# A delta-rule recurrence with a soft mixture of experts: each PSUM bank to one engine at a time in the plan, and half of the query masks by ScalarE and GpSimd

## The chip, the cores and the metric

The kernel runs on one core of one Trainium2 chip. The metric is the device time in microseconds (us) of one execution. The engines are TensorE (PE in the profile; its weight loads are PEld), VectorE (DVE), ScalarE (ACT), GpSimd (POOL) and SyncE (SP), which issues nearly all DMAs. Each engine works through its own queue in order; semaphores tie the queues together. TensorE writes to PSUM, which has 8 banks of 512 float32 columns on 128 partitions; everything else lives in one SBUF tile.

## The reference, cut to what matters

```python
# attention: batch 4, heads 8, 768 tokens, head size 48
k_n = k / (norm(k) + 1e-6)
for t in range(S):
    y[:, :, t] = einsum('bhd,bhde->bhe', q[:, :, t], state)
    v_old = einsum('bhde,bhd->bhe', state, kt)
    state = state + bt * einsum('bhd,bhe->bhde', kt, vt - v_old)
# soft mixture of experts on x (3072 x 384): 8 experts, 4 slots each, F = 1024
logits = x @ phi
d = softmax of logits over the tokens;  slot_input = d.T @ x
slot_out[e] = maximum(slot_input[e] @ w1[e], 0) @ w2[e]
c = softmax of logits over the slots;   out = c @ slot_out
```

## The kernel before

The recurrence is worked in 12 chunks of 64 tokens, all 32 heads together. Two chunks make a pair g (0 to 5). For a chunk n:

- `load_kq`, `load_v` (L470, L485) bring K, Q and V. `turn` (L535) transposes them on TensorE, eight 128x128 blocks at a time, and L546 copies the result out of PSUM.
- `gram` (L560) multiplies keys with keys, and keys with queries, per head. Its output tile has two banks, one for each index i. `keys` copies the key part out with a mask (ScalarE L587 and L585; VectorE L583 for the lower part of chunks 0 and 1); `queries` masks the query part on VectorE (L600) into `AT`. For chunks below `APART` = 4 keys and queries have tiles of their own, later ones share one tile for each half of the heads. `pack` (L625; VectorE for chunks 0 and 1, else GpSimd) gathers the diagonal blocks of the pair in `Gd`.
- `invert(g)` inverts the 16x16 diagonal blocks of the pair on VectorE: a transpose (L677), the norms of the keys (L690, Ln and Exp on ScalarE L694 and L695, reciprocals L707 and L709, small products on GpSimd L700 to L706), a scaling (L717), 15 columns of a multiply and a subtract (L727, L731), and transposes back (L749, L757). GpSimd spreads the result (L766).
- `join(n)` builds the inverse of the 64x64 block: L793, products L802, L820, L853, L864 with their copies L810, L826, L832, L843, L856, L869, and at the end the fix of the far part, L874 (`fix64`), into `Zs`.
- `step(n)` is the recurrence: `ks` (L910) reads the state, L917 subtracts from V, `qs` (L929) gives the first part of Y, `w` (L942) is the solution U, which ScalarE copies to `cU` (L956). GpSimd copies its second half with the partition halves exchanged to `cU2` (L962), because in `AT` the heads of the second half lie on the other partitions. `sup` (L982) adds to the state in PSUM (`pS`, two banks of its own), ScalarE copies it out (L988), and `au` (L1003) adds the second part of Y, copied out by L1013. In the last step the U copies are split between ScalarE and VectorE by partition half, each over its 384 columns (L956, L966), and Y is made in two parts.
- `route(n)` transposes Y (L1038, copy L1045) and makes the slot logits (L1063, copy L1069). `phase` (L1111 to L1152) keeps a running softmax over the tokens and adds up the slot inputs (L1141, L1150); it runs after chunks 3, 7, 10 and 11.

After the last step come `top` and `t3` (L1242, the slot inputs turned), the first expert products (`first`, L1267, with relu L1274 and L1276 and transposes L1283), the second ones (L1300), and for each half of the columns the sum over experts (L1311) and the product with the combine weights (L1322), copied out by L1324 and stored by L1326. `combine(g)` makes these combine weights: a transpose (L1081), a softmax (L1085 to L1094) and a transpose back (L1096, copy L1098). The weights of the experts are loaded by L1207 (w1) and L1217 (w2).

No order is written by hand. `Plan` collects every operation with its engine, an assumed duration, and the buffers it reads and writes. `schedule` is a list scheduler that runs at build time: it keeps a clock for each engine, takes the ready operation whose remaining path plus `key` is largest, gives it addresses in SBUF and PSUM, and emits the operations in the order of their assumed start. `SHIFT` adds a number to the key of each kind of operation; `SLACK` lengthens the path of one copy of the state (L988, upper half). `after=` in `op` orders an operation in the plan without any data behind it. Where the plan expects TensorE to be idle, it puts a filler product (L453) into a spare bank: `pl.spare` names the state's banks until the state is first written, later a bank must be free. The semaphores that the program really waits on are derived from what the emitted instructions read and write, banks of PSUM included, not from the plan's clock.

Of the kernel before, what the change touches and what calls it, by code (L numbers as in the profile page):

```python
# [16 lines left out]
SLACK = 0.00  # L17
HEAD = 40.0
SHIFT = {
    0: -43.2, 1: 38.7, 2: 22.3, 3: 23.9, 4: -10.2, 5: 9.8, 6: -5, 7: 3.3, 8: 43.6, 9: -36.4,  # L20
    10: -3.7, 11: -70.3, 12: -18.3, 13: -15.3, 14: 18, 15: 69.1, 16: -83.2, 17: 34.4, 18: 17.4,
    19: -17, 20: -10, 21: -21.3, 22: -80.1, 23: -24.9, 24: -39.6, 25: 33.2, 26: 46.2, 27: -4.5,
    28: -53.6, 29: 26.6, 30: 3.1, 31: 116.3, 32: -19.1, 33: 72.8, 34: -27.9, 35: 43, 36: -12.6,
    37: 27.4, 38: 21.6, 39: 25.9, 40: 38.2, 41: -12.1, 42: -52.9, 43: 39.8, 44: 1.5, 45: -59.4,
    46: 13.1, 47: 11.7, 48: -54.3, 49: -6.2, 50: -27.4, 51: -21.7, 52: 29.9, 53: 29.9, 54: 25.4,
    55: -86.9, 56: -75.3, 57: -1.3, 58: 40.6, 59: 2.6, 60: 52.3, 61: -1, 62: 67.4, 63: -21.5,
    64: 22.5, 65: 6.7, 66: -2.6, 67: -23.8, 68: 23.2, 69: -36.6, 70: -61.2, 71: -15.8, 72: 20.5,
    73: 6.7, 74: -41.5, 75: 10.7, 76: 35.5, 77: 5.4, 78: -50.1, 79: 17.8, 80: 9.7, 81: -3.2,
    82: -26.6, 83: 3.5, 84: -32.5, 85: 17.6, 86: 49.6, 87: -45.4, 88: 19.9, 89: -10, 90: 40.2,
    91: -5.8, 92: 0.9, 93: -0.8, 94: 15.1, 95: 11.2, 96: -14.5, 97: 10.1, 98: -8.6, 99: -89.6,  # L30
    100: -11.5, 101: -13.4, 102: -12.3, 103: -17.7, 104: -1.7, 105: -15.2, 106: 3.4, 107: 20,
    108: 11.8, 109: 2, 110: -1.4, 111: -52.5, 112: 10.9, 113: 31.5, 114: -40.9, 115: -2.6,
    116: -46.4, 117: -32.5, 118: -6.7, 119: -62.2, 120: 45.1, 121: -27.1, 122: 3.7, 123: -25.1,
    124: 2.8, 125: -25.9, 126: -75.6, 127: 27.6, 128: 83.5, 129: 62.8, 130: 32.4, 131: 55.6,
    132: 26, 133: -75.5, 134: -118.6, 135: -56.5, 136: 63.1, 137: 73.4, 138: -3.2, 139: -5,
    140: -7.2, 141: -54.1, 142: -41.2, 143: 6.1, 144: 77.3, 145: 22.9, 146: -19.4, 147: 20.7,
    148: -48.2, 149: 44.3, 150: 17.8, 151: 27, 152: 62.3, 153: 14.5, 154: -12.8, 155: -21.7,
    156: 10.5
# [13 lines left out]
class Op:  # L52
    def __init__(self, eng, dur, fn, lat, key):
        self.eng, self.dur, self.fn, self.lat, self.key = eng, dur, fn, lat, key
        self.deps, self.outs, self.bufs = {}, [], {}
        self.start = self.done = None
        self.path = self.slack = 0.0
        self.port = False

# [58 lines left out]
class Plan:  # L118
# [22 lines left out]
    def op(self, eng, dur, fn, r=(), w=(), after=(), lat=0.0, key=0.0, keep=0, ni=8, ut=300.0, port=False):  # L141
# [10 lines left out]
        for mode, regs in (("r", r), ("w", w)):  # L152
            for reg in regs:
                b, part = reg if isinstance(reg, tuple) else (reg, None)
                b.uses.append((o, part, mode))
        for a in after:
            if a is not None:
                o.deps[a] = None
# [16 lines left out]
    def schedule(self):  # L175
# [3 lines left out]
        live = {False: [], True: []}  # L179
        wait = {o: len(o.deps) for o in self.ops}  # L180
# [20 lines left out]

        busy = {"DVE": 0.0, "POOL": 0.0}
# [3 lines left out]
        while left:  # L206
# [13 lines left out]
            for x in cand:  # L220
                o = x[1]
                t = max(free[e], x[0])
                new = [b for b in o.bufs if b.addr is None]
# [20 lines left out]
                if e == "PE":  # L244

                    while self.filler:
# [9 lines left out]
                        b.addr = self.spare[0].addr if self.spare[1].start is None else room(b, at, 0)  # L256
# [19 lines left out]
                order.append(o)  # L276
                left -= 1
# [30 lines left out]
def kernel(  # L308
# [18 lines left out]
    P = 128  # L327
# [246 lines left out]
    def keys(n, j0, nj, ps, w):  # L574
        def ev(y, lower):
            dve = lower and n < 2

            def go():
                i_ = A(ps).rearrange("p i (y j f) -> p i y j f", j=4, f=w)[:, :, y - j0 // 4, :, 0:C].rearrange(
                    "p i j (b t) -> p i j b t", b=2)  # L580
                o = G3(n)[:, 8 * y:8 * y + 8].rearrange("p (i j) b t -> p i j b t", i=2)
                if dve:
                    nc.vector.tensor_scalar(o[:, :, :, 1], i_[:, :, :, 1], M1(), None, op0=ALU.mult)  # L583
                elif lower:
                    nc.scalar.activation(o[:, :, :, 1], i_[:, :, :, 1], ACT.Copy, scale=M1())  # L585
                else:
                    nc.scalar.activation(o[:, :, :, 0::2], i_, ACT.Copy, scale=M0())  # L587
            pl.op("DVE" if dve else "ACT", (t_dvp(256) if dve else t_act(256)) if lower else 0.60, go, r=[ps, cm0],
                  w=[(Gk[n], (lower, y))])
        for y in range(j0 // 4, (j0 + nj) // 4):  # L590
            ev(y, 0)
            ev(y, 1)
# [3 lines left out]
    def queries(n, j0, nj, ps, w):  # L596
        x = lambda: A(ps).rearrange("p i (y j f) -> p i y j f", j=4, f=w)[:, :, 0:nj // 4, :, w - C:w]
        for y in range(nj // 4):
            def cut(y=y):
                nc.vector.tensor_tensor(  # L600
                    x4(A(AT[n]), j0, nj, C)[:, :, y], x()[:, :, y],
                    A(cmA).unsqueeze(1).unsqueeze(1).broadcast_to([P, 2, 4, C]), op=ALU.mult)
            pl.op("DVE", 0.70, cut, key=-50, r=[ps, cmA], w=[(AT[n], y + j0 // 4)])
# [51 lines left out]
    def invert(gs):  # L655
# [51 lines left out]
        pl.op("DVE", 0.25, lambda: V.reciprocal(A(rn), A(nrm)), r=[nrm], w=[rn])  # L707
        pl.op("POOL", 0.89, norm, r=[ssq], w=[nrm, rn], port=True)
        pl.op("DVE", 0.25, lambda: V.reciprocal(A(rn), A(nrm)), r=[nrm], w=[rn])  # L709
# [173 lines left out]

    cS, cU, cU2 = pl.buf(32 * D), pl.buf(32 * D), pl.buf(16 * D)
    for t in (cU, cU2, cS):
        pl.op("POOL", t_ps(t.size), lambda t=t: nc.gpsimd.memset(A(t), 0.0), w=[t], key=20)

    def step(n):
# [58 lines left out]
        U2 = lambda: A(cU2).rearrange("p (i j f) -> p i j f", i=2, j=4)  # L947
        last = n == N - 1

        def uev(c):  # L950
            def go():
                o = A(cU).rearrange("p (y x c d) -> p y x c d", y=2, c=2, d=D)[ha(c), :, :, c]
                x = A(pW)[ha(c), :, 0:8 * D].rearrange("p y (x d) -> p y x d", d=D)
                if last:
                    o, x = o[:, 0], x[:, 0]
                (nc.vector.tensor_copy if c and last else nc.scalar.copy)(o, x)  # L956
            return go

        def uev2(c):
            def go():  # L960
                if not last:
                    nc.gpsimd.tensor_copy(  # L962
                        A(cU2).rearrange("p (x c d) -> p x c d", c=2, d=D)[ha(c ^ 1), :, c],
                        A(cU).rearrange("p (y x c d) -> p y x c d", y=2, c=2, d=D)[ha(c), 1, :, c])
                    return
                (nc.vector.tensor_copy if c and last else nc.scalar.copy)(  # L966
                    A(cU2).rearrange("p (x c d) -> p x c d", c=2, d=D)[ha(c ^ 1), :, c],
                    A(pW)[ha(c), 1, 0:8 * D].rearrange("p (x d) -> p x d", d=D))
            return go
        for f, b, cols in ((uev, cU, 384 if last else 768), (uev2, cU2, 384)):  # L970
            for c in H2:
                if b is cU2 and not last:
                    pl.op("POOL", t_po(384), f(c), r=[(cU, c)], w=[(b, c)], port=True)
                    continue
                dve = c and last
# [383 lines left out]
```

## Time and profile before

| | |
|---|---|
| median of 3 runs | 290.08 us (289.23 to 290.38) |
| profiled execution | 289.64 us, of which the span is 287.9 us |
| mean granted TensorE clock | 0.966 |
| start of solution L942 of chunk 0, 1, 2, 3 | 48.65, 64.33, 84.75, 99.0 us |
| of chunk 4, 5, 6, 7 | 120.08, 138.64, 152.25, 175.21 us |
| of chunk 8, 9, 10, 11 | 188.04, 201.08, 216.88, 226.80 us |
| t3 (L1242) ends, last L1300 starts, last output is issued | 240.05, 270.70, 284.3 us |

The span is cut in 40 equal slices; each digit is the busy share of a slice in tenths, and PEclk is the granted TensorE clock in tenths of full speed:

```profile
PE   8998899698988989989998989988897999999870
DVE  3789989778768957998769877987241387320440
PEclk9999999799999999999999999999999997999965
DMA  8999954808509293370766601489999999999596
```

VectorE is full in the early slices and fills again whenever a pair is inverted; after slice 27 it is mostly idle. DMA is full in the first slices (K, Q and V of the first chunks) and from slice 27 on (the experts' weights). The clock drops in slice 8, in the expert products, and at the end.

### The profile page before, as it was taken

The page shows a single profiled execution, that of the slowest core. Times are in us where ns is not written, and L with a number is a line of the kernel's source. Part 1 is how long each engine was busy: PE and PEld are TensorE (multiplying, and loading weights), DVE is VectorE, ACT ScalarE, POOL GpSimd, SP SyncE. Part 2 cuts the span into 40 slices and gives each one's busy share as a digit, 9 for nine tenths or more (in the row PEclk, how much of TensorE's full clock was granted, in tenths as well). Part 3 has the DMA queues.
Part 4 walks back from the last instruction along what each step waited for, and adds up shares of the span by engine and source line. Part 5 has one row for each costly group of instructions (what it writes and reads, how often), then busy time and mean ns, then how long its engine had stood idle before and what let it go on. Part 6 is the DMA issues. An engine that isn't in the chain of part 4 may idle for free.

```text
span 287.9 us, 13776 instructions
## 1 busy us (share of the span) xinstructions
PE 252.9 (88%) x6040; PEld 212.5 (74%) x6040; DVE 191.6 (67%) x438; ACT 149.8 (52%) x279; POOL 119.3 (41%) x288
## 2 busy tenths in 40 slices
PE   8998899698988989989998989988897999999870
PEld 6887788697878878688888879877786764367650
DVE  3789989778768957998769877987241387320440
ACT  5484386358557486359656856563645352201430
POOL 8943058705943377715952677417422000000000
PEclk9999999799999999999999999999999997999965
DMA  8999954808509293370766601489999999999596
GB/s 103 141 138 138 137 82 59 124 4 106 65 5 123 46 133 40 59 112 3 91 80 77 93 2 31 109 203 338 384 355 297 318 315 322 329 305 314 170 293 223
DMA packets 105836, 45.12 MB, mean 157 GB/s; under 512 B 77009, under 2 KB 99569, under 8 KB 105777
## 3 DMA queue, kind: packets, MB, share of 16 engines
q1 hardware_dynamic: 105600, 44.05, 71.1%
q8 instruction: 47, 0.77, 1.2%
q10 hardware_dynamic: 48, 0.10, 0.2%
q0 software_dynamic: 128, 0.10, 0.2%
q14 instruction: 13, 0.10, 0.2%
HBM read 39.52 MB, written 4.72 MB: 154 GB/s over the span
## 4 chain that ended last, share of the span: by engine, by line
PE 37%; DVE 30%; POOL 10%; issue 7%; ACT 7%; DMA 5%; SPq 1%; DVEq 0%; ACTq 0%; POOLq 0%
DVE sb L727 6%; DVE sb L731 5%; PE pb L1267 4%; PE pb L1300 4%; PE pb L1322 3%; DVE sb L832 3%; PE pb L535 3%; PE pb L982 3%; PE pb L929 3%; DMA sb<-in_q_dram 2%; POOL sb L843 2%; POOL sb L625 2%; DVE sb L600 2%; POOL sb L766 2%; DMA sb<-in_k_dram 2%
## 5 line engine op out<-in xcount | busy, mean ns | idle before, releaser
L843 POOL COPY sb<-sb 32x128 f32<-32x128 f32 x96 | 30.2, 315 | 19.7 <-DVE sb L826 12.2
L546 ACT ACTIVATE sb<-pb 128x1024 f32<-128x1024 f32 x23 | 22.9, 1023 | 10.7 <-PE pb L535 10.4
L766 POOL COPY sb<-sb 32x256 f32<-32x256 f32 x44 | 19.6, 445 | 20.3 <-DVE sb L757 18.4
L731 DVE TENSOR_TENSOR sb<-sb 128x30 f32<-128x30 f32 (+7 forms) x90 | 25.8, 287 | 3.1
L727 DVE TENSOR_TENSOR sb<-sb 128x30 f32<-128x30 f32 (+7 forms) x90 | 26.2, 291 | 2.4
L560 PE MATMUL pb<-sb 48*64 48x128 f32 (+1 forms) x1024 | 25.7, 247 | 1.7 <-DVE sb L600 1.1
L535 PE MATMUL pb<-sb 128*128 128x128 f32 x192 | 24.6, 276 | 1.8 <-DMA sb<-in_q_dram 1.0
L956 ACT COPY sb<-pb 64x768 f32<-64x768 f32 (+1 forms) x23 | 17.9, 779 | 14.8 <-PE pb L942 9.9
L560 PEld LDWEIGHTS pb<-sb 48*64 48x64 f32 x1024 | 22.0, 134 | 4.0 <-ACT sb L546 1.4
L982 PE MATMUL pb<-sb 128*48 128x96 f32 x352 | 18.4, 259 | 6.5 <-ACT sb L956 5.1
L988 ACT ACTIVATE sb<-pb 64x768 f32<-64x768 f32 x22 | 17.7, 805 | 11.7 <-PE pb L982 11.5
L535 PEld LDWEIGHTS pb<-sb 128*128 128x128 f32 x192 | 20.9, 141 | 3.6 <-issue 1.6
L982 PEld LDWEIGHTS pb<-sb 128*48 128x48 f32 x352 | 15.9, 130 | 8.6 <-ACT sb L956 7.0
L600 DVE TENSOR_TENSOR sb<-pb,sb 128x512 f32<-128x512 f32 x24 | 15.8, 685 | 8.5 <-ACT sb L587 5.2
L1003 PE MATMUL pb<-sb 128*64 128x96 f32 x384 | 19.1, 250 | 0.9 <-DVE sb L966 0.5
L453 PE MATMUL pb<-sb 128*128 128x256 f32 (+2 forms) x74 | 18.2, 383 | 1.1 <-DVE sb L422 1.1
L1003 PEld LDWEIGHTS pb<-sb 128*64 128x64 f32 x384 | 17.2, 140 | 1.8 <-DVE sb L966 0.7
L587 ACT ACTIVATE sb<-pb,sb 128x512 f32<-128x512 f32 x24 | 15.8, 686 | 5.1 <-PE pb L560 3.6
L962 POOL COPY sb<-sb 64x384 f32<-64x384 f32 x22 | 12.5, 566 | 12.8 <-ACT sb L956 12.3
L929 PE MATMUL pb<-sb 128*64 128x96 f32 x352 | 16.9, 249 | 0.6 <-DVE sb L917 0.6
L910 PE MATMUL pb<-sb 128*64 128x96 f32 x352 | 16.9, 249 | 0.5 <-ACT sb L988 0.4
L832 DVE STREAM_TRANSPOSE sb<-sb 64x512 f32<-64x512 f32 x24 | 16.9, 703 | 0.5
(158 smaller groups left out, 523.3 us busy)
## 6 DMA issues: line engine op xcount, KB each, us to landing
sb<-in_moe_w_dram SPq DMA_DIRECT2D x48, 256.0 KB, 5.4
sb<-in_moe_w_dram SPq DMA_DIRECT2D x32, 384.0 KB, 6.2
sb<-in_k_dram SPq DMA_DIRECT2D x24, 192.0 KB, 4.7
sb<-in_v_dram SPq DMA_DIRECT2D x48, 96.0 KB, 4.6
sb<-in_q_dram SPq DMA_DIRECT2D x24, 192.0 KB, 6.0
out_dram<-sb SPq DMA_DIRECT2D x24, 192.0 KB, 2.4
sb<-in_beta_dram ACTq DMA_DIRECT2D x1, 96.0 KB, 4.9
sb<-in_moe_phi_dram POOLq DMA_DIRECT2D x2, 32.0 KB, 4.4
```

The lines of the kernel that those rows point to most:

```text
L535: nc.tensor.transpose(o[:, 128 * j:128 * j + 128], A(src)[:, 128 * j:128 * j + 128], ident())
L546: nc.scalar.activation(o, x, ACT.Copy)
L560: mm(A(ps)[ha(c ^ (j // 4)), i, w * (j - j0):w * (j - j0) + w], kq(n)[hd(i), j, c, 0:C], kq(n)[hd(i), j, c, lo:hi])
L600: nc.vector.tensor_tensor(x4(A(AT[n]), j0, nj, C)[:, :, y], x()[:, :, y], A(cmA).unsqueeze(1).unsqueeze(1).broadcast_to([P, 2, 4, C]), op= ...
L727: V.tensor_tensor(p, blk(tt, j, j + 1, 0, m).broadcast_to(sh), blk(lb, j, j + 1, j + 1, 16).rearrange("p x a i -> p x i a").broadcast_to(s ...
L731: V.tensor_tensor(t, t, p, op=ALU.subtract)
L766: e(o[64 * i + 32 * u:64 * i + 32 * u + 32, :, c, :, u], x[64 * c + 32 * u:64 * c + 32 * u + 32, :, i])
L832: pl.op("DVE", t_dv(512), lambda: nc.vector.transpose(A(t32).rearrange("p (x z t) -> p x z t", z=2, t=32)[ha(c), :, c], Z()[ha(c)]), r=za, ...
L843: nc.gpsimd.tensor_copy(o[q:q + 32, :, c, i], zx()[64 * c + 32:64 * c + 64, y, i].rearrange("p (j t) -> p j t", t=32))
L929: mm(ypart(j)[:, :, c], kq(n)[:, j, c, C:2 * C], S0()[:, j, c], start=b % 2 == 0 and c == 0)
L982: mm(A(pS)[hd(i), j // 4, a:a + 2 * D], A(Kb[n])[:, 128 * j + 64 * i:128 * j + 64 * i + D], U0()[:, j // 4, i, j % 4], start=n == 0 and j ...
L1003: mm(ypart(j)[:, i], A(AT[n])[:, C * xi(i, j):C * xi(i, j) + C], (U2()[:, i, j % 4] if j > 3 else U0()[:, 0, i, j % 4]), start=n == 0 and ...
```

## The change

- **The plan and PSUM banks.** `op` notes which PSUM buffers an operation touches, and with which part. `schedule` gets `turn`: an operation whose buffer is at that moment in use by another engine is put back until that engine is done, unless the two name different parts.
- **Keys of chunks 0 and 1** are copied by bank: ScalarE takes bank i = 0, VectorE bank i = 1, each two upper parts of 256 columns and one lower part of 256. Later chunks are copied as before; the assumed duration of a 512-column copy goes from 0.60 to 0.68.
- **Queries.** The first half of the heads is masked by VectorE as before. The second half is copied by ScalarE from PSUM to a buffer `qt` (512 columns), and GpSimd applies the mask from there with two `affine_select` of 64 partitions x 512, which also exchange the partition halves. The second half of U then needs no exchange: `cU2`, its 22 GpSimd copies and its memset are gone.
- **Last solution.** Bank 0 is copied by ScalarE, bank 1 by VectorE, each in two partition halves; each part of `au` waits for its own bank only.
- **Combine** is emitted after the first expert products, ordered behind t3 (L1242) instead of behind the last solution.
- **Fillers** may use the state's banks again once the last solution is done.
- The priorities of the last steps' `route` and `phase` change, `SLACK` goes from 0 to 7.15, two reciprocals are assumed to take 0.34 instead of 0.25, and `SHIFT` has 169 new numbers for 157 old ones. All queues get a new order through this, SP's among them.

```diff
-SLACK = 0.00
+SLACK = 7.15
 SHIFT = {
...
@@ op
+                if b.psum:
+                    o.reads.append((b, part))
@@ schedule
+        turns = {}
+
+        def turn(o, t):
+            last = None
+            for b, part in o.reads:
+                for p, q in turns.get(b, ()):
+                    if p.eng != o.eng and p.done + self.SEM > t and (q is None or part is None or q == part):
+                        t, last = p.done + self.SEM, p
+            return t, last
...
+                late, p = turn(o, t)
+                if p is not None:
+                    x[0], o.behind = late, p
+                    continue
...
-                        b.addr = self.spare[0].addr if self.spare[1].start is None else room(b, at, 0)
+                        free_ = self.spare[1].start is None or self.spare[2].start is not None
+                        b.addr = self.spare[0].addr if free_ else room(b, at, 0)
...
+                for b, part in o.reads:
+                    turns.setdefault(b, []).append((o, part))
@@ keys
-            pl.op("DVE" if dve else "ACT", (t_dvp(256) if dve else t_act(256)) if lower else 0.60, go, r=[ps, cm0],
-                  w=[(Gk[n], (lower, y))])
-        for y in range(j0 // 4, (j0 + nj) // 4):
-            ev(y, 0)
-            ev(y, 1)
+            c = 512 if i is None and not lower else 256
+            pl.op("DVE" if i else "ACT", t_dvp(c) if i else 0.68 if c == 512 else t_act(c), go, r=[(ps, i), cm0],
+                  w=[(Gk[n], (lower, y, i)) for y in ys])
+        for i in H2 if n < 2 else (None,):
+            for y in range(j0 // 4, (j0 + nj) // 4):
+                ev((y,), i, 0)
+                if i is None:
+                    ev((y,), i, 1)
+            if i is not None:
+                ev(H2, i, 1)
@@ queries
+        if j0 + nj == 8:
+            qt = pl.buf(512)
+            pl.op("ACT", 0.61, lambda: nc.scalar.activation(
+                A(qt).rearrange("p (i j f) -> p i j f", i=2, f=C), x(1), ACT.Copy), r=[ps], w=[qt])
+            for c in H2:
+                def cut(c=c):
+                    nc.gpsimd.affine_select(
+                        out=A(AT[n])[ha(c), 512:1024].rearrange("p (x t) -> p x t", t=C),
+                        in_=A(qt)[ha(c ^ 1)].rearrange("p (x t) -> p x t", t=C),
+                        compare_op=ALU.is_ge, fill=0.0, base=-1, pattern=[[0, 8], [1, C]], channel_multiplier=-1)
+                pl.op("POOL", 0.65, cut, r=[qt], w=[(AT[n], (1, c))], port=True)
@@ step
-        for f, b, cols in ((uev, cU, 384 if last else 768), (uev2, cU2, 384)):
+        for y in H2 if last else (None,):
             for c in H2:
...
+                cols = 384 if last else 768
+                pl.op("DVE" if y else "ACT", t_dvp(cols) if y else t_act(cols), uev(y, c), r=[(pW, y)],
+                      w=[(cU, (u, c)) for u in (H2 if y is None else (y,))])
...
-                               (U2()[:, i, j % 4] if j > 3 else U0()[:, 0, i, j % 4]),
+                               U0()[:, j // 4, i, j % 4],
@@ body
-        pl.bias = -11.5 * (N - 1 - n) + 4
+        pl.bias, pl.part = (-11.5 * (N - 1 - n) + 4, 0) if n < N - 2 else (-6.0, 1)
...
-    for g in range(NG):
-        combine(g)
...
     first(0)
     first(1)
+    for g in range(NG):
+        combine(g, [ot3])
...
+    pl.spare += (chain[N - 1],)
```

## The prediction

> **What bounds the kernel now.** I read the page first: whole-span shares, then the tail of the chain of waits, then TensorE's queue step by step.
>
> ```profile
> span 287.9 us, 13776 instructions
> PE 252.9 (88%) x6040; PEld 212.5 (74%) x6040; DVE 191.6 (67%) x438; ACT 149.8 (52%) x279; POOL 119.3 (41%) x288
> ```
>
> TensorE is busy 88%, but 18.2 us of that are filler matmuls (L453), nearly all before 50 us. So the mean hides three stages: a head (to the first solution, L942, at 48.65), twelve recurrent steps, and a tail from 228. The windows cut at the starts of the solutions show the middle:
>
> ```profile
> 48.60:64.30 15.70, 13.20 (x322) 12.34 (x313) 11.62 (x30) 6.76 (x8) 7.26 (x17) 0.89 0.51 72
> 64.30:84.80 20.50, 18.29 (x510) 16.20 (x506) 15.21 (x29) 12.88 (x22) 12.91 (x32) 1.00 0.50 61
> 188.00:201.10 13.10, 10.96 (x306) 9.38 (x302) 10.79 (x26) 6.29 (x11) 6.01 (x13) 1.00 0.93 271
> ```
>
> Columns: window, length, then busy PE, PEld, DVE, ACT, POOL, clock, DMA share, GB/s. Counted from the queue with the mean duration of each group (w 1.12, sup 1.55, au, ks and qs 1.48, Y transposes 0.82, eight input transposes 1.06, sixteen 64x128 Gram products 1.06, L802 1.07, L820 1.00, L853 and L864 0.63), the eleven steps from w0 to w11 hold 161.5 us of TensorE work in 178.15 us. The idle 16.6 is what a better order can win there. The first step alone loses 3.9 (15.7 against 11.8):
>
> ```profile
> 52.94 0.47 PE L864 MATMUL pb<-sb 64*64 64x64 f32 x17 [2.15 <-issue]
> 53.33 2.80 PE L982 MATMUL pb<-sb 128*48 128x96 f32 x32
> ```
>
> 2.15 us without a named releaser, and then sup takes 2.80 instead of 1.55, in the only early window with a clock under 1. The head is bound by VectorE (27.88 busy of 30 from 20 to 50), whose column loop (L727, L731) is interrupted:
>
> ```profile
> 22.25 1.37 DVE L727 TENSOR_TENSOR sb<-sb 128x96 f32<-128x96 f32 x1
> 22.22 1.29 POOL L625 TENSOR_TENSOR sb<-sb 128x512 f32<-128x512 f32 x1 [3.10 <-ACT sb L585]
> 26.71 1.28 DVE L600 TENSOR_TENSOR sb<-pb,sb 128x512 f32<-128x512 f32 x2
> ```
>
> A column multiply that takes 0.26 elsewhere takes 1.37 while GpSimd packs, and two query masks sit between columns. ScalarE and VectorE also wait for each other where both read one Gram tile:
>
> ```profile
> DVE sb L600 <- ACT sb L587: 5.2, 6, 2.7
> ACT sb L585 <- DVE sb L600: 4.2, 6, 0.8
> PE pb L982 <- ACT sb L956: 5.1, 6, 1.3
> ```
>
> The last solution is read by the two engines strictly in turn, 2.3 us for four copies:
>
> ```profile
> 228.07 0.48 ACT sb L966
> 228.65 0.57 DVE sb L966
> 229.24 0.57 DVE sb L956
> 229.88 0.48 ACT sb L956
> 230.41 0.88 PE pb L1003 x16
> ```
>
> **The change, part by part.** The base is the profiled execution's own 289.64 (span 287.9 and 1.74 around it), which is 0.44 below the median 290.08.
>
> The rule "one engine per bank at a time" adds no wait: the mutual waits above are already in the program. It only makes the plan place instructions where they will really run. Its price is nothing; its worth is the order.
>
> **Queries.** VectorE loses 12 of 24 L600 (12 x 0.685 = 8.2) and gets 0.8 back in the keys of chunks 0 and 1 (six copies of 256 at 0.48 for four L583 at 0.52): 7.4 less. ScalarE gets 12 copies of 512 from PSUM, between 0.58 (L1285) and 0.69 (L587); I take 0.6, 7.2 in all, on an engine busy 52%. GpSimd loses 22 copies L962 (566 ns, 12.5 us) and gets 24 masks of 64x512, a shape that is not in the trace: between 0.57 (L962, 64x384) and 1.29 (L625, two inputs). AFFINE_SELECT goes from 0.19 (128x8) to 0.30 (128x128), which by slope gives 0.64 at 512: 24 x 0.64 = 15.4. The third 384-wide copy of U into cU2 disappears from the path to au (L1003), but there the sup product already stands between, so this saves nothing on the path. [...]
>
> **Head: 3.3 later.** In the new VectorE order the norms (L690, L707, L709) come after both packs and the spread. From the end of the squares at 11.64: eviction 1.21, six key copies 2.9, packs 2.06, spread 1.25, small ones 0.8, to 19.8; then nothing covers Ln and Exp, two reciprocals, 0.9 and 0.6 on GpSimd, a copy and the scale (0.69), together 3.6, so the columns begin near 23.5 instead of 20.73: +2.8. Before, keys and packs covered those waits. The columns last 12.84 now: 8.2 of their own, four L600 (2.56), 2.1 of stretch by two packs. The L600 go behind the columns; six masks come in on GpSimd at about 0.5 of stretch each (L962 beside columns at 154.43 cost two of them 0.18 and 0.33). 8.2 + 2.1 + 3.0 = 13.3: +0.4. From there to the first fix64 (L874) I add the new order's rows to 14.3 against 14.2: +0.1. w0 starts at 48.65 + 3.3 = 51.9. The fillers agree in direction: the head has two more of 256 columns.
>
> **First step: 5.5 shorter.** Between w0 and w1 the new queue has 9.6 of work instead of 11.8 (two groups of input transposes go to the next step), and I assume that the 2.15 wait and the slow clock do not return. The floor is the recurrence itself: w10 to w11, with little else, takes 9.92. I take 10.2, so w1 at 62.1 instead of 64.33.
>
> **w1 to w9: 3.4 less idle.** Work there is 127.7 (0.5 of it a filler) in the new queue, 127.3 in the old one; the old time is 136.75, idle 9.45. The new order alternates light steps (10.5 to 11.8) with heavy ones (17.6 to 22.3), and puts eight transposes (1.06) or more behind nearly every solution and often again behind sup, where L982 waits for the 1.6 of two U copies. VectorE has 5.5 less to do here; its loop for one pair of chunks sums to some 30.6 against 33 of TensorE. Bounds: nothing and 9.45. I take a little over a third, 3.4, since 0.6 of each U eviction stays uncovered and not all of the idle is there. w9 at 62.1 + 127.7 + 6.1 = 195.9 instead of 201.1.
>
> **w9 to w11: 0.8 more.** The new queue leaves both joins of the last pair behind w9: 24.4 of work instead of 22.4. Adding the rows along w9, sup, ks, L802, L820, L853, L864, fix64 gives 16.5 to w10, then 10.0: 26.5 against 25.7. w11 at 222.4 against 226.8.
>
> **Tail: 0.6 less.** The two banks of the last solution are copied side by side (2 x 0.48 and 2 x 0.57); but 0.65 of logits and two fillers stand before au, so au ends 3.05 after w11's end against 3.29. Without the combine transposes (L1081) and VectorE's softmax in between, the slot products (L1242) end about 1.0 earlier relative to w11; this includes the 0.24. The transposes come back, nine at 0.15 to 0.17 inside the dense products of L1267 and L1300, less 0.9 of fillers that stood there: +0.4. VectorE and ScalarE are idle there (5.8 and 2.9 busy of 14), so the softmaxes are hidden.
>
> Sum: +3.3 - 5.5 - 3.4 + 0.8 - 0.6 = -5.4: 289.64 - 5.4 = 284.2, as a median 284.7.
>
> **Rivals.** (A) The stall at w0 returns: it has no releaser, so no order need remove it. 284.7 + 3.9 = 288.6. For it: "issue" waits recur elsewhere (1.32 at 204.7). Against: the instructions at that place are others. (B) The weights hold the tail. The last w2 transfer is issued at 262.0 and takes 6.2, the last L1300 starts at 270.70; DMA is full from 200 to 254 (0.99 to 1.06). If they start no earlier, only 2.5 can be won: 287.6. Against: they wait for buffers that the steps free, and so move along. (C) Slower: the masks hold VectorE's columns. At the upper price 1.29 each stretches a column by 1.0 (L731 took 1.25 beside an L625). That is 6 x 0.5 = 3.0 more in the head, and 4 x 0.5 = 2.0 more in the first step, where four masks run beside columns that stand ahead of fix64 of chunk 1. In the later steps four masks a pair cost 4.0 where 1.5 of stretch is reckoned above, so VectorE's loop comes to 33.1, TensorE's own length, and no idle is won: 284.7 + 3.0 + 2.0 + 3.4 = 293.1. It decides from about 1.0 us a mask. For it: the stretched rows, and that nothing of this shape is in the trace. Against: AFFINE_SELECT's small slope.
>
> **How the numbers follow.** Forecast 0.50, A 0.15, B 0.10, C 0.25. The forecast's own range is 280 to 288 (idle won between 0 and 8). The range on record goes from 279.5 (nearly all of the 9.45 won) to 292.8, just short of C. With 0.5% (1.45 us) as what can be told from no change: faster 0.50 + 0.10 + a third of A = 0.65; same two thirds of A and 0.02 of C = 0.12; slower 0.23.
>
> **What would show it.** Right: first solution near 52, second near 62, last near 222; L600 halved; masks near 0.64; columns in the head uninterrupted by L600 yet stretched; last solution's copies side by side. Wrong: masks over 1 us, first-step sup again near 2.8, or idle before sup as before.

## The result: 0.9% slower, and the profile after

The changed kernel takes 292.73 us (median of 4 runs) against 290.17 for the kernel before: a ratio of 1.0091 (95% interval 1.0061 to 1.0120). The forecast was 284.7. A second measurement of the pair (e10) gave 1.0073 (1.0026 to 1.0119). The profiled execution took 292.89, its span is 291.2. Executions more than 1.5% above the fastest of their kernel count as slow and are left out of the ratios (here one of 301.96), but the profiles of e1, e3, e6, e13 and e14 below are of such executions.

The page of the changed kernel, its span, busy times and granted clock by fortieths:

```profile
span 291.2 us, 13840 instructions
...
PE 260.9 (90%) x6064; PEld 219.6 (75%) x6064; DVE 184.8 (63%) x428; ACT 155.8 (54%) x293; POOL 123.5 (42%) x289
...
PEclk9999799999999999999999999979997999999975
```

VectorE lost 6.8 us of work and the kernel still got slower. The groups of instructions (busy us, mean ns of one, then the idle time before them and its releaser) show that the new work costs what was estimated, 0.64 and 0.6:

```profile
L644 POOL TENSOR_SCALAR_AFFINE_SELECT sb<-sb 64x512 f32<-64x512 f32 x24 | 15.6, 655 | 9.9 <-ACT sb L640 8.7
L640 ACT ACTIVATE sb<-pb 128x512 f32<-128x512 f32 x12 | 7.1, 592 | 4.1 <-PE pb L584 4.0
```

So rival C, masks that take 1.29 us each, is out by its own price. Where the time went is read from the starts of the solutions (L942 before, L986 after). The repeats come from e9 and e10; e8 has the changed kernel's instructions up to the last solution.

| us | forecast | before, again | after, again | e8 |
|---|---|---|---|---|
| first solution w0 | 51.9 | 48.65, 48.75 | 53.70, 53.74 | 51.18 |
| first step, w0 to w1 | 10.2 | 15.68, 15.80 | 11.14, 11.14 | 11.16 |
| w1 to w9 | 133.8 | 136.75, 136.87 | 137.64, 136.91 | 137.50 |
| w9 to w11 | 26.5 | 25.72, 27.65 | 30.20, 28.99 | 30.35 |
| w11 to the span's end | 60.5 | 61.1, 61.0 | 58.5, 58.8 | 57.5 |

In the profiled pair the five rows add to 5.05 - 4.54 + 0.89 + 4.48 - 2.6 = 3.3, the difference of the spans. The windows of the changed kernel for the first two steps and for the step before w9 (columns as in the prediction: window, length, busy PE, PEld, DVE, ACT, POOL, clock, DMA share, GB/s):

```profile
53.70:64.80 11.10, 9.86 (x294) 8.84 (x294) 9.67 (x24) 5.78 (x8) 9.30 (x19) 1.00 0.79 115
64.80:83.60 18.80, 17.68 (x474) 15.66 (x470) 12.79 (x26) 11.89 (x19) 10.96 (x26) 1.00 0.63 68
187.80:202.40 14.60, 12.49 (x305) 10.77 (x301) 10.79 (x31) 7.40 (x12) 7.03 (x17) 0.88 0.65 180
```

The first step has lost its stall and its low clock (1.00 for 0.89); its sup takes 1.53 instead of 2.80:

```profile
56.58 1.53 PE L1011 MATMUL pb<-sb 128*48 128x96 f32 x32 [0.33 <-ACT sb L999]
```

The step to w9 has a low clock instead (0.88, where the kernel before had 1.00), behind a wait of L898 for VectorE of 1.96 us; in the repeat (e10) that step kept its clock (1.00) and took 14.1. The last solution is copied by two engines side by side, as forecast (timelines of ScalarE and VectorE):

```profile
233.91 0.47 ACT L999 COPY sb<-pb 64x384 f32<-64x384 f32 x1 [1.78 <-PE pb L986]
...
233.92 1.12 DVE L999 COPY sb<-pb 64x384 f32<-64x384 f32 x2 [2.44 <-PE pb L986]
```

Behind the head, the stage from w9 to w11 shows the largest loss. VectorE's big transpose of the last pair, before:

```profile
195.41 1.96 DVE L749 STREAM_TRANSPOSE sb<-sb 128x1024 f32<-128x1024 f32 x1
```

and after, with GpSimd's copies behind it:

```profile
207.85 1.98 DVE L794 STREAM_TRANSPOSE sb<-sb 128x1024 f32<-128x1024 f32 x1
...
210.81 4.13 POOL L811 COPY sb<-sb 32x256 f32<-32x256 f32 x8
...
216.94 2.71 POOL L888 COPY sb<-sb 32x128 f32<-32x128 f32 x8 [1.09 <-DVE sb L871]
```

Before, the pair's columns are done 5.7 us ahead of w9 (201.08); after, 5.4 us behind it (202.48). What follows them then lies between w9 and w10: the transposes, eight copies on GpSimd, and the products of `join`.

### The profile page after: what moved, and what is told of

Read it like the earlier page. It is cut to its first block, busy times and chain, and to the rows that moved or that the text cites. A ratio compares the mean times of both kernels' runs of the same rounds, so it can differ in the third digit from the quotient of the medians.

```text
span 291.2 us, 13840 instructions
## 1 busy us (share of the span) xinstructions
PE 260.9 (90%) x6064; PEld 219.6 (75%) x6064; DVE 184.8 (63%) x428; ACT 155.8 (54%) x293; POOL 123.5 (42%) x289
## 4 chain that ended last, share of the span: by engine, by line
PE 47%; POOL 16%; DVE 15%; ACT 8%; issue 7%; DMA 4%; SPq 1%; DVEq 0%; POOLq 0%; ACTq 0%
POOL sb L888 5%; POOL sb L811 5%; PE pb L584 4%; PE pb L1328 4%; PE pb L1293 4%; PE pb L477 4%; PE pb L954 3%; PE pb L1350 3%; ACT sb L615 3%; PE pb L1032 3%; PE pb L986 2%; PE pb L559 2%; PE pb L1011 2%; DVE sb L776 2%; DVE sb L772 2%
## 5 line engine op out<-in xcount | busy, mean ns | idle before, releaser
L888 POOL COPY sb<-sb 32x128 f32<-32x128 f32 x96 | 31.0, 323 | 12.3 <-DVE sb L871 6.1
L838 POOL COPY sb<-sb 64x256 f32<-64x256 f32 x22 | 9.4, 429 | 53.2 <-DVE sb L794 36.8
L615 ACT ACTIVATE sb<-pb,sb 128x256 f32<-128x256 f32 (+1 forms) x46 | 24.8, 566 | 9.5 <-PE pb L584 8.5
L584 PE MATMUL pb<-sb 48*64 48x128 f32 (+1 forms) x1024 | 26.8, 248 | 2.0 <-issue 1.6
L999 ACT COPY sb<-pb 64x768 f32<-64x768 f32 (+1 forms) x24 | 18.4, 765 | 17.9 <-PE pb L986 12.3
L776 DVE TENSOR_TENSOR sb<-sb 128x30 f32<-128x30 f32 (+7 forms) x90 | 25.9, 288 | 3.1
L559 PE MATMUL pb<-sb 128*128 128x128 f32 x192 | 26.9, 286 | 0.4 <-issue 0.2
L772 DVE TENSOR_TENSOR sb<-sb 128x30 f32<-128x30 f32 (+7 forms) x90 | 24.7, 275 | 2.6
L477 PE MATMUL pb<-sb 128*128 128x256 f32 (+2 forms) x98 | 24.5, 386 | 1.3 <-DVE sb L446 1.1
L559 PEld LDWEIGHTS pb<-sb 128*128 128x128 f32 x192 | 21.9, 146 | 2.7 <-issue 0.9
L477 PEld LDWEIGHTS pb<-sb 128*128 128x128 f32 x98 | 19.2, 220 | 4.8 <-DVE sb L446 1.1
L811 POOL COPY sb<-sb 32x256 f32<-32x256 f32 x44 | 20.6, 469 | 2.9 <-DVE sb L802 0.6
L1011 PEld LDWEIGHTS pb<-sb 128*48 128x48 f32 x352 | 15.8, 130 | 7.4 <-ACT sb L999 7.2
L1032 PE MATMUL pb<-sb 128*64 128x96 f32 x384 | 18.7, 249 | 1.8 <-issue 1.1
L644 POOL TENSOR_SCALAR_AFFINE_SELECT sb<-sb 64x512 f32<-64x512 f32 x24 | 15.6, 655 | 9.9 <-ACT sb L640 8.7
L1075 ACT ACTIVATE sb<-pb 128x768 f32<-128x768 f32 x11 | 8.9, 811 | 16.4 <-PE pb L1068 16.3
L954 PE MATMUL pb<-sb 128*64 128x96 f32 x352 | 16.7, 248 | 0.9 <-ACT sb L1017 0.5
```

The costliest lines, as they stand in the source:

```text
L477: pl.filler = lambda b, w: mm(A(b)[:, 0, 0:w].rearrange("p (a f) -> p a f", f=min(w, P)), A(cone), A(cone)[:, 0:min(w, P)].unsqueeze(1).br ...
L559: nc.tensor.transpose(o[:, 128 * j:128 * j + 128], A(src)[:, 128 * j:128 * j + 128], ident())
L584: mm(A(ps)[ha(c ^ (j // 4)), i, w * (j - j0):w * (j - j0) + w], kq(n)[hd(i), j, c, 0:C], kq(n)[hd(i), j, c, lo:hi])
L615: nc.scalar.activation(o, i_, ACT.Copy, scale=m)
L772: V.tensor_tensor(p, blk(tt, j, j + 1, 0, m).broadcast_to(sh), blk(lb, j, j + 1, j + 1, 16).rearrange("p x a i -> p x i a").broadcast_to(s ...
L776: V.tensor_tensor(t, t, p, op=ALU.subtract)
```

## The experiments

Three theories. O: the plan's new order lost the time, above all by the late last pair. M: the queries' way over ScalarE and GpSimd lost it. D: stretches of low clock, which fall differently in each execution, make up part of the differences. Ratios are to the kernel before, run on the same chip. They are less exact than their intervals: the kernel before against itself (e9) gave 0.9939 (0.9888 to 0.9991), so differences under some 0.6% are not told apart.

### The masks: e1, e2, e5

```diff
 e1
-    A(qt).rearrange("p (i j f) -> p i j f", i=2, f=C), x(1), ACT.Copy), r=[ps], w=[qt])
+    x4(A(AT[n]), 4, 4, C)[:, :, 0], x(1), ACT.Copy), r=[ps], w=[qt])
...
-    out=A(AT[n])[ha(c), 512:1024].rearrange("p (x t) -> p x t", t=C),
+    out=A(AT[n])[ha(c), 512:520], in_=A(AT[n])[ha(c), 512:520],
...
 e2
-    pl.op("ACT", 0.61, lambda: nc.scalar.activation(
+    pl.op("ACT", 0.61, lambda: nc.vector.tensor_tensor(
+        x4(A(AT[n]), 4, 4, C)[:, :, 0], x(1), A(cmA)..., op=ALU.mult), r=[ps], w=[qt])
...
-    nc.gpsimd.affine_select(
+    pass
...
 e5, e2 and in gram
-    mm(A(ps)[ha(c ^ (j // 4)), i, ...], kq(n)[hd(i), j, c, 0:C], kq(n)[hd(i), j, c, lo:hi])
+    for a, b, h in ([(lo, C, c ^ 1), (C, hi, c)] if lo < C < hi and j > 3 else
+                    [(lo, hi, c ^ (j // 4 if lo < C else 0))]):
+        mm(A(ps)[ha(h), i, ...], kq(n)[hd(i), j, c, 0:C], kq(n)[hd(i), j, c, a:b])
```

> The changed kernel in its own order, with one edit: ScalarE writes the half of the query products straight into AT, and each of the 24 GpSimd masks (L644) treats 64x8 instead of 64x512. It leaves out nearly all of the mask and the exchange of the partition halves for that half of the queries. Theory O (the new order lost the time: the last pair is prepared a step later): the masks lie beside other work but for the head, where two stand ahead of the first pair's copies (37.55 to 38.9) and four stretch columns; 0.5 to 1.5 less, so 291.0 to 292.3, and w9 to w11 stays at 29.5 to 30.2. Theory M (the masks on GpSimd lost it, by their 15.6 us and by holding VectorE): 4.5 or more less, 288 or below.

> The changed kernel in its own order, with the masks given back to VectorE: at the place of ScalarE's copy (L640) VectorE multiplies by the mask from PSUM, and the 24 GpSimd masks are not issued. It leaves out the exchange of the partition halves for that half of the queries. VectorE gets 12 x 0.69 = 8.3 us back, ScalarE loses 7.2, GpSimd 15.6. Theory O: the move of the queries is not what lost the time, so undoing it alone wins nothing: 292 to 295. Theory M: 288 to 290, as before the change.

> The edit of e2 made whole, in the changed kernel's order: VectorE masks the second half of the queries, and so that no exchange of partition halves is needed, the products of keys and queries with j over 3 are split in two of 64x64, the queries into their own half. Nothing is left out. Theory M, as e2 left it (the queries' way over ScalarE and GpSimd holds the first pair's copies, the first step and the norms of the last pair): first solution near 51.5, first step near 10.2, last solution some 4 before the changed kernel's; the split products cost 0.1 a chunk, 0.8 in all; 0.985 to 0.992 of before. Theory O alone (order only, the masks no cost): 1.005 to 1.015.

Measured: e1 0.9967 (0.9931 to 1.0002), e2 0.9872 (0.9820 to 0.9923), e5 0.9978 (0.9939 to 1.0017). Against 1.0073 to 1.0091 for the changed kernel, e1 and e5 are about 1% better, e2 2%; why e2 is so far below e5 is not settled (their own medians are close, 290.21 and 290.47; the kernel before took 292.28 beside e2 and 290.86 beside e5). Neither theory hit: the masks cost more than O allowed, and w9 to w11 stayed at 30.3 (e2) and 30.0 (e5), which M alone would not leave. Two places show part of the 1%. The first step takes 10.2 to 10.5 instead of 11.1 (though e6 and e13, whose first solution was 6 us late, had 10.4 with their masks), and the step to w9 12.9 to 13.4 instead of 14.1 to 14.6, where masks no longer stand ahead of the norms in GpSimd's queue. In the changed kernel, at the step to w9 (GpSimd, VectorE and TensorE):

```profile
188.69 0.66 POOL L644 TENSOR_SCALAR_AFFINE_SELECT sb<-sb 64x512 f32<-64x512 f32 x1
189.43 0.25 POOL L745 TENSOR_TENSOR sb<-sb 128x32 f32<-128x32 f32 x1
...
190.34 0.35 DVE L754 RECIPROCAL sb<-sb 128x32 f32<-128x32 f32 x1 [0.96 <-POOL sb L747]
...
191.59 1.08 PE L898 MATMUL pb<-sb 128*32 128x64 f32 x32 [1.96 <-DVE sb L877]
```

and in e2 the same product:

```profile
188.32 0.65 PE L896 MATMUL pb<-sb 128*32 128x64 f32 x32 [1.10 <-DVE sb L875]
```

The price of 0.655 each was right; here the masks (and a memset between them) stand in GpSimd's queue ahead of work that is due: L745 starts at 189.43, behind the second mask. In the head they look as if they did the same. GpSimd's timeline in the changed kernel and in e2:

```profile
37.55 1.36 POOL L644 TENSOR_SCALAR_AFFINE_SELECT sb<-sb 64x512 f32<-64x512 f32 x2 [5.00 <-ACT sb L640]
38.95 1.69 POOL L811 COPY sb<-sb 32x256 f32<-32x256 f32 x4
```

```profile
37.28 1.70 POOL L809 COPY sb<-sb 32x256 f32<-32x256 f32 x4 [11.38 <-DVE sb L800]
```

In the first, L802 is done at 37.29 and L811 starts 1.7 later, behind two masks that themselves waited for ScalarE. But this is the work of a stretch of low clock (0.69 from 32 to 36 us), which e2's profile does not have and which is followed further below. In e8, whose masks are the same and whose clock is 1.00 there, the masks start at 35.80 and the copies at the time of e2:

```profile
37.23 1.69 POOL L812 COPY sb<-sb 32x256 f32<-32x256 f32 x4
```

So at a clock of 1.00 the masks cost the head nothing.

### The rule and the fillers: e4, e8

e4 puts `turn` and its use into the kernel before. e8 leaves the fillers behind the last solution out:

```diff
         for o in order:
-            o.fn()
+            if o.seq >= 0 or o.start < self.spare[2].start:
+                o.fn()
```

> The kernel before with one edit: the plan gives each PSUM bank to one engine at a time, as in the change (its SHIFT and every instruction stay). Theory O: the rule adds no wait, but every later choice of the plan falls otherwise, and the SHIFT found for the old choices no longer fits: slower than before, 293 to 300. The rival, my prediction's own step (the rule makes the plan place instructions where they really run, and its worth is a better order): 288 to 290, no slower than before.

> The changed kernel without its fillers (L477) behind the last solution. Theory F (the tail's gain of 2.6, where 0.6 was forecast, is the clock: fillers in the state's banks keep it up ahead of the first expert products): the 96 first products take 12.0 to 12.5 us again instead of 10.5, tail 60 to 60.5, 1.014 to 1.018 of before. Rival (it comes from moving the combine transposes behind L1268, which closes the gaps): products at 10.5, tail within 0.5 of 58.5, 1.006 to 1.011.

e4: 1.0216 (1.0165 to 1.0267), and w1 to w9 takes 145.4 instead of 136.8. The rule by itself makes the kernel slower, though it adds no work but eight fillers: every choice after the first changed one falls otherwise, and the old SHIFTs do not suit them. e8: 1.0108 (1.0029 to 1.0187); its 96 first expert products (the line that is L1293 in the changed kernel) take 10.51 in one piece with and without fillers, and the tail is 57.5. So the fillers are not what the tail won. Moving the combine transposes is left as a cause that was not tried alone, and part of the gain is luck: kernels whose instructions behind w11 are those of the changed kernel take 58.1 to 62.6 there (58.1 in e7, 60.3 in e5, 60.9 in e2, 62.6 in e17), against 61.1 and 61.0 before. A wait of TensorE without a releaser goes with it, in the changed kernel and in e17:

```profile
236.92 1.07 PE L1032 MATMUL pb<-sb 128*64 128x96 f32 x21 [1.07 <-issue]
```

```profile
236.83 1.87 PE L1040 MATMUL pb<-sb 128*64 128x96 f32 x20 [2.58 <-issue]
```

In e17 the 96 first products behind it take 11.79, against 10.51 in the changed kernel.

### Repeats: e9, e10

> The kernel before, unchanged, for a second profile. So far the profiles show one or two stretches in which the granted clock falls, at places that differ from one execution to the next of the same instructions. Theory D (the first step's 15.7, its wait of 2.15 and sup's 2.80 are the work of such a stretch and not of the order): a second execution has a first step near 12 to 13.5, or the stretch elsewhere. My prediction's own step (the order makes it): 15.5 again, with sup at 2.8. Time ratio 1.00.

> The changed kernel, unchanged, for a second profile beside the kernel before on this chip. Theory D: first solution near 51.2 where no low clock falls into the head, 53 or more where it does; w9 to w11 at 30 in either case. Theory M as far as the head goes: 53.5 again. Time 1.004 to 1.012 of before.

The first step of the kernel before is 15.80 again, with 2.37 of waiting without a releaser and sup at 2.80 again: it belongs to the order, and theory D falls there. In the head D holds. w0 is 53.7 in both profiles of the changed kernel and 51.2 in e8 and e11, whose instructions are the same up to there. With the masks on VectorE it is likewise 51.5 to 51.8 where the six fillers and eight transposes of the rows below take 1.56 and 1.04 (e2, e5, e16), and 53.2 and 54.0 where they take 2.59 and 1.73 (e7) and 2.33 and 1.91 (e17). TensorE's timeline, the changed kernel and then e8:

```profile
29.92 0.56 PE L584 MATMUL pb<-sb 48*64 48x64 f32 x19 [1.42 <-issue]
30.41 2.30 PE L477 MATMUL pb<-sb 128*128 128x256 f32 x6
32.51 1.91 PE L559 MATMUL pb<-sb 128*128 128x128 f32 x8
```

```profile
29.73 0.56 PE L585 MATMUL pb<-sb 48*64 48x64 f32 x19 [1.14 <-issue]
30.23 1.56 PE L478 MATMUL pb<-sb 128*128 128x256 f32 x6
31.62 1.04 PE L560 MATMUL pb<-sb 128*128 128x128 f32 x8
```

Behind the wait the clock falls in the first and stays in the second (windows of both, the clock third from the end):

```profile
32.00:36.00 4.00, 4.00 (x46) 3.50 (x48) 3.58 (x13) 1.02 (x1) 0.56 (x1) 0.69 0.94 111
```

```profile
32.00:36.00 4.00, 3.92 (x82) 3.51 (x80) 3.48 (x13) 1.62 (x2) 0.62 (x2) 1.00 0.92 118
```

The six fillers and the eight transposes then take 4.0 instead of 2.4, and the queries of the next chunk, their masks and the first pair's copies all come later: 2.5 at w0. The length of the wait does not decide whether the clock falls: in e2, behind the same 1.42, the six fillers take 1.56 as in e8; in e7, behind 1.02, they take 2.59.

### The last pair by hand: e3, e6, e7, e11, e13, e16, e17

All keep the plan and move single instructions in its list afterwards:

```diff
         order = self.schedule()
+        for m in moves:
+            self.move(order, *m)
...
-    e = nc.scalar.copy if head and u else nc.gpsimd.tensor_copy
+    e = nc.scalar.copy if (head or g == 5) and u else nc.gpsimd.tensor_copy
```

The second edit (four of the eight L811 to ScalarE, and likewise four L888) is in all but e3. e7, e16 and e17 stand on e5, the others on the changed kernel.

> The changed kernel with five instructions of the last pair (chunks 10 and 11) moved by hand after the plan is made, and nothing else: one mask (L644) and the memset L727 go behind the norms L745 to L751 on GpSimd, the fix64 of chunk 9 (L919) goes behind the second column on VectorE, L1180 behind the last transposes, and L802 ahead of L794. Theory O: the waits of VectorE for GpSimd at 190.3 (0.96), for L909 at 196.5 (1.59) and for L1171 at 205.8 (1.20) shrink, and the eight L811 start some 2 us earlier against the end of L794; w9 to w11 goes from 30.2 to some 27.5, the time to 289.5 to 291. Theory M and any theory in which this stage only follows from a lack of engine time: no change, 292 to 293.

> The changed kernel with its GpSimd masks, and only the last pair treated by hand: the memset L727 behind the norms, L919 of chunk 9 behind the second column, L1180 behind the last transposes (as in e3, but L794 stays ahead of L802), and ScalarE, idle there, takes four of the eight L811 of the last pair and four of the eight L888 of chunk 10. Theory O for this stage (the chain VectorE columns, L794, L802, L811, mo16 sets the tenth solution): columns 1.7 earlier, L811 2.0 shorter, L888 0.5 shorter; w9 to w11 from 30.2 to 26 to 27, time 0.995 to 1.000 of before. Rival (TensorE's queue and the recurrence set this stage, the copies only fill it): w9 to w11 at 29 or more, 1.006 to 1.010.

> e5 and e6 together; nothing is left out. If the two losses are separate, as M for the head and O for the last pair have it, the gains add: first solution near 51.5, w9 to w11 at 26 to 27, 0.970 to 0.982 of before. If one wait only takes the place of the other, no better than the better of the two.

> The changed kernel with the last pair treated by hand once more. In e6 and e7 ScalarE's four copies of L811 stood behind L1075, and L847 on TensorE behind L954 and L1068, so one wait took the place of another. Now L847 goes ahead of L1068 and L954, the eight L811 and the copies L855 ahead of ScalarE's L1075, the first L865 ahead of L973. Theory O for this stage (places in the queues set the tenth solution): L865 starts 2 us earlier against w9, w9 to w11 at 26.5 to 28.0 and the time 1.5 to 3 less than the changed kernel's. Rival (engine time or the recurrence sets it): 29.5 or more.

> The changed kernel with the moves of e11, and on TensorE the second L847 directly behind the first L865, L898 and L909 of chunk 10 ahead of the second L865, the logits L1093 between. Theory O for this stage (places in TensorE's queue set the tenth solution): L865 to w10 in 6.0 to 6.8 us instead of 9.4 in e11, w9 to w11 at 26.5 to 27.5, the time 2.5 to 3.5 less than the changed kernel's: 0.997 to 1.001 of before. Rival (the stage is set by engine time): w9 to w11 at 29 or more, 1.004 or more.

> e5 and the moves of e13 together, the rest in the changed kernel's order; nothing is left out. If the two losses are separate, 1% from the masks and 0.9% from the last pair: 0.982 to 0.992 of before.

> e16 with one more move: L919 of chunk 10 ahead of the second L871 on VectorE. In e16 the last L909 ended at 215.36 and L919 began at 216.94. Theory O for this stage: w9 to w10 at 17.4 to 17.8 instead of 18.9, w9 to w11 at 27.4 to 27.9; the time 1 us less than e16's, 0.986 to 0.996 of before. Rival (engine time): w9 to w11 at 28.8 again.

Measured, each against its own w9 (first two columns: the pair's transposes into zd (L794) start, its first mo16 product (L865) starts, but for two of its matmuls in the first two rows):

| us from w9 | transposes | mo16 | w10 | w11 | ratio (95%) |
|---|---|---|---|---|---|
| changed kernel | +5.4 | 12.5 | 19.5 | 30.2 | 1.0091 (1.0061 to 1.0120) |
| e3 | +4.8 | 11.9 | 19.6 | 30.6 | 1.0045 (1.0005 to 1.0084) |
| e6 | +3.7 | 12.1 | 19.2 | 29.9 | 1.0020 (0.9971 to 1.0069) |
| e7 | +3.7 | 12.9 | 19.6 | 29.7 | 0.9993 (0.9952 to 1.0033) |
| e11 | +3.7 | 10.4 | 19.8 | 30.6 | 1.0016 (0.9958 to 1.0074) |
| e13 | +3.7 | 10.4 | 18.8 | 28.8 | 1.0013 (0.9968 to 1.0059) |
| e16 | +3.7 | 10.5 | 18.9 | 28.9 | 0.9991 (0.9940 to 1.0043) |
| e17 | +3.7 | 10.5 | 18.4 | 28.7 | 1.0053 (1.0016 to 1.0090) |
| e12, e18 (below) | -4.6 | 4.5, 4.4 | 17.1 | 28.5, 28.0 | |
| before, e9 | -5.7 | | 15.8, 16.9 | 25.7, 27.7 | |

None won the 2.5 to 4 us that were expected; from w9 to w11 it was the rivals' value that came in e6, e11 and e17, and nearly in e13. Each time the wait moved to the next queue of the same chain. In e3 GpSimd's first copies waited for the transposes that now came second. In e6 and e7 ScalarE's four copies stood behind its copy of Y. In e11 the product L898 stood on TensorE behind the other chunk. In e16, on VectorE, the last fix of chunk 10 (L927) stood behind the first fix of chunk 11 (L879), which waited for its product:

```profile
216.54 0.48 DVE L879 SCALAR_TENSOR_TENSOR sb<-pb,sb 128x256 f32<-128x256 f32 x1 [3.98 <-PE pb L873]
216.94 0.74 DVE L927 SCALAR_TENSOR_TENSOR sb<-sb,pb 128x512 f32<-128x512 f32 x1
```

(L879 and L927 are L871 and L919 of the changed kernel.) In e17 the solution of chunk 10 waited for a ScalarE copy instead. From the start of the zd transposes to w10 it takes 14.1 to 16.1 us in all eight. So the start of those transposes goes with the length of the stage: in the table, columns done behind w9 go with 18.4 to 19.8 to w10, columns done ahead of it with 15.8 to 17.1. (e2, +5.0 and 20.3, and e15, -2.1 and 17.3, fit; e14, +2.3 and 20.9, does not.) That the stage follows from it was not shown alone, since no run moved the whole preparation and left the rest as it was. That e17 measured slower than e16 with a shorter stage is not explained; in the profiles its first solution comes 2.5 later and its tail is 3.7 longer; the six fillers of the head take 2.33 in e17 and 1.56 in e16, the 96 first products 11.79 and 10.50, and the mean granted clock is 0.972 and 0.989.

### Other orders of the same instructions: e12, e14, e15, e18

```diff
 SHIFT = {
-    0: -8.6, 1: -29.8, 2: -1.6, 3: -2.5, 4: -29.3, ...
+    0: -16.7, 1: -95.7, 2: -95, 3: -3.9, 4: 8.2, ...
```

> The changed kernel with other numbers in SHIFT and nothing else: they were looked for with the kernel's own plan, whose planned end falls from 280.6 to 271.1 (274.2 for the kernel before). Every instruction, its engine and the rule stay. Theory O (what lost the time is the order that these SHIFTs give, the last pair above all; by the plan, w9 to w11 is 24.1 instead of 30.0 and the first solution at 48.6 instead of 50.5): 0.972 to 0.990 of before. Theory M (GpSimd's masks and ScalarE's copies cost more than VectorE wins, in whatever order): 1.000 or more.

> The kernel before with the rule (as e4) and SHIFTs from a search as long as that for e12; planned end 273.6, e12's 271.1, the kernel before's own 274.2. Theory O: the time follows the order, whatever the structure: 0.980 to 1.000 of before, within 1% of e12. Theory M (the queries' new way costs): clearly below e12, under 0.980.

> The change with all query masks on VectorE (the structure of e5, planned as such) and SHIFTs from a search as long; planned end 273.1. Theory O: 0.980 to 0.998, within 1% of e12. Theory M: the masks cost some 1% in e1 and e5 and do so here: 0.970 to 0.980.

> The order of e12 with the edit of e5: at the places of ScalarE's copies (L640) VectorE masks, the split products, no masks on GpSimd; nothing is left out. Theory M2 (the queries' new way costs 1% in whatever order it stands): 0.973 to 0.982 of before. Theory O (it costs where the order puts it ahead of work that is waited for, and e12's order does so less): 0.983 to 0.992, as e12.

Planned ends are the kernel's own reckoning, not times; here they are beside what the chip made of them:

| kernel | SHIFTs | planned end | ratio (95%) |
|---|---|---|---|
| e4, before with the rule | of before | 284.3 | 1.0216 (1.0165 to 1.0267) |
| changed kernel | its own | 280.6 | 1.0091 (1.0061 to 1.0120) |
| before | its own | 274.2 | 1 |
| e14, before with the rule | searched | 273.6 | 1.0012 (0.9964 to 1.0060) |
| e15, masks on VectorE | searched | 273.1 | 0.9895 (0.9802 to 0.9988) |
| e12, changed kernel | searched | 271.1 | 0.9875 (0.9812 to 0.9938) |
| e18, e12 and the edit of e5 | of e12 | | 0.9788 (0.9732 to 0.9844) |

e12 has the changed kernel's instructions and rule, but for 16 fillers fewer, which the plan places, and is 2% faster than it by order; e4 and e14 differ by the same 2%. That the order can cost or win that much is what theory O says, and it is shown. That it is "above all" the late last pair is not: of the 3.0 us between the profiles of e12 and e10, 0.5 lie in w9 to w11 (28.5, where the plan had 24.1), while w0 comes 4.0 earlier (1.5 against e8 and e11, whose clock is 1.00 there) and the first step is 1.7 longer. e14 and e12 lie 1.4% apart, a little more than O's bound of 1%, with the one planned to end later being the slower; one search each does not tell a better structure from a luckier search. e18 (285.50 against 291.29 us) is the fastest of all: the edit of the masks, worth about 1% in the changed kernel's order, is worth 0.9% in e12's, as theory M2 had it (0.973 to 0.982), though the intervals of e12 and e18 overlap. In the profiles e18's w1 to w9 is 132.0, against 136.7 in e12 and 136.8 before. Part of that lies in e12's third step, where sup takes 2.25 and au 2.47 (1.53 and 1.49 in e18); the granted clock from 48.6 to 228 us is 0.97 in e12 and 0.98 in e18.

## Why the prediction was wrong

The sign was wrong. By its steps:

- **The rule.** "It only makes the plan place instructions where they will really run. Its price is nothing; its worth is the order." The first half held, no new wait of that kind showed. The worth was negative with the old SHIFTs (e4), and the new SHIFTs give a worse order than others for the same instructions (e12). This is the step that failed first: the new order got credit for idle time without being followed. The next two terms are where the credit stood.
- **w1 to w9, 3.4 less idle.** Failed: 137.64 and 136.91, no idle won. "A little over a third" of 9.45 had no mechanism behind it, only bounds. In the profiled execution the masks took some of it: the norms of the last pair stood behind them and L754 waited 0.96 at 190.3.
- **w9 to w11, 0.8 more.** Failed: +4.5 in the profiled pair, +1.3 to +4.6 over the repeats. The rows of TensorE were added up as if TensorE alone set the stage. The same view had said that both joins of the last pair lie behind w9; VectorE's queue for that pair would have shown its columns ending there too.
- **Head, 3.3 later.** Right at a clock of 1.00, with some luck: 51.2 (e8, e11) against 51.9 forecast. In e8 the columns begin at 24.84 instead of 23.5 but last 11.05 instead of 13.3, since the masks stretch four columns by 0.33 to 0.40 (by 0.38 to 0.49 in the profiled execution) and only one pack stretches one, by 0.97. From their end to w0 it takes 15.3 against 15.1 before, close to the "+0.1". The other 2.5 of the profiled execution is the stretch of low clock, 0.69 from 32 to 36 us.
- **First step, 5.5 shorter.** Right in kind, 4.5: the wait and the slow sup did not return, so rival A fell. It is 0.9 longer than forecast, and e2 and e5 without the masks are 0.7 to 0.9 shorter.
- **Tail, 0.6 less.** Right in sign in the profiled pair, 2.6, and in the repeats, 2.2; but over the profiles with the same end the tail takes 58.1 to 62.6, so the size is partly luck. Before, the first expert products ran at a lower clock in one of two executions (0.89 from 239 to 254 us; 1.00 from 240 to 256 in e9); in the changed kernel's two, in neither (10.51 us in both). The weights (rival B) did not hold it.
- **Rival C**, the masks hold the columns, gave nearly the measured time by a wrong price. The masks' way costs about 1% at 0.655 each, in two orders; the places at the first step and at the step to w9 show part of it, the rest is not located. One mask took 0.655 against 0.685 for VectorE's L634, which also has 512 columns but reads PSUM; but it takes two of them, 1.31 together, to mask as much as one L634.
- **The sum.** Its line left out the 0.4 of added TensorE work that its own w1 to w9 term held.

## What to carry to other kernels

When a scheduler decides the order, a structural edit and a new order come together, and the order can be worth more than the edit: make the edit in the old order and the new order without the edit, or the sign of either stays unknown. Cost a moved instruction by who stands behind it in its engine's queue, not by its duration. Before giving a stage credit, follow every engine's part of the work that the stage ends on; removing one wait of a chain mostly shows the next one.

## What the runs showed of the hardware

Executions of the same instructions up to the first solution differ by 2.5 us there: 53.70 and 53.74 (changed kernel, e10) against 51.18 and 51.22 (e8, e11). Behind a wait of TensorE the granted clock between 32 and 36 us is 0.69 and 0.75 in the first two and 1.00 in the others. The places differ too: the changed kernel's step to w9 has a clock of 0.88 in one profile and of 1.00 in the other. TensorE was busy 2.58 of the 4.00 us from 28 to 32 in the changed kernel, and its clock fell; in e2 it was busy 2.59 there, and its six fillers took 1.56, as in e8. So neither the wait nor the busy time in that stretch decides it, and what does is not shown.

Fillers stand in TensorE's queue as well: where the clock fell, six of them took 2.30 instead of 1.56, and the transposes behind them started at 32.51 instead of 31.62.
